# Expert weights loaded in fewer transfers with longer runs, in a fused attention and feed-forward kernel

## The chip, the cores and the metric

The kernel runs on one core of a Trainium2 chip. A core has five engines with instruction streams of their own: TensorE (PE, with weight loads shown apart as PEld), VectorE (DVE), ScalarE (ACT), GpSimd (POOL) and SyncE (SP). They meet through semaphores. Data comes from the chip's memory by DMA: here POOL issues all loads that turn float32 into float16 on the way, and SP issues the rest (stores, transposes, copies within the on-chip memory). The metric is the device time of one execution in microseconds; lower is better.

## What is computed

Attention over 8 batches with 8 heads of size 64: 512 local rows see 32 global columns and a band of 32 to each side; 32 global rows see everything. Its output, 4352 rows of 512 numbers, goes through a feed-forward layer whose activation is `h * clip(h + 3, 0, 6) / 6`.

```python
s_g = scale * q_g @ concat(k_g, k_l).T;  out_g = softmax(s_g) @ concat(v_g, v_l)
s_ll = where(abs(i - j) <= 32, scale * q_l @ k_l.T, -1e9)
out_l = softmax(concat(scale * q_l @ k_g.T, s_ll)) @ concat(v_g, v_l)
x = concat(out_g, out_l) as 4352 x 512
h = x @ w_in                       # w_in  512 x 2048
g = h * clip(h + 3, 0, 6) / 6
out = g @ w_out                    # w_out 2048 x 512
```

The inputs are float32; the kernel works in float16 with float32 sums.

## The kernel before

**A planner writes the order.** The kernel describes its work as operations with an engine (or a choice of engines), a cost, dependencies and a rank. `Plan.run` plays these through an event model and so fixes the order in which every engine gets its instructions; the code is then emitted in that order by hand (`tc.manual_schedule`). Each engine runs its own list strictly in order. So any change of a cost or a rank moves instructions on all engines, far from the edit. The semaphore waits are not the planner's: they are added when the program is built, from the regions of the tiles that instructions write and read.

**Loads.** `load` (L343) is a DMA issued by POOL, with a price from `dma(rows, run)` (L331): so many rows, each a run of so many bytes of float32. POOL's loads go through one queue, first in, first out, and at most eight are under way: a ninth waits for the first to land. The order of the first loads is the list `ORDER` (L379), read by `nth`: `k0 q0 v0 v1` are batch 0's, `K Q V G` batch 1's, `w0` to `w3` the quarters of w_in, `o0` to `o7` the eighths of w_out, `id` and `bd` the identity and the mask band.

**Weights.** `weights_in` (L637) loads w_in by quarters of its columns: 512 columns for each of the 512 rows, which are folded into 4 x 128 partitions, so 512 runs of 2 KB. `weights_out` (L643) loads w_out by 256 rows at a time, 256 runs of 2 KB.

**The feed-forward layer.** The 2048 hidden columns are cut into 16 groups of 128. `first` (L946) computes one group for up to 512 rows of x: four matmuls (L953) whose stationary side is a 128 x 128 piece of w_in, then a ReLU on ScalarE (L959) and a gate on VectorE (L963) that writes `g`. `second` (L970) multiplies all 16 groups with w_out (L979), four at a time. `ffn_local` (L1003) runs `first` for the 16 groups of a batch, for batch 0 in two halves of 256 rows; a group of w_in's quarter c depends on that quarter through `wi[c // (NDFF // 4)]` (L1012). `ffn_global` (L1028) does the 256 global rows at the end.

**Around the start.** Until the first x is ready, PE runs filler matmuls on the identity (L1094, `warm`), so that its clock stays up. Batch 0's attention uses scores (L769), maxima with the mask (L781), exponentials (L785), transposes of the probabilities (L798), products with v (L812), normalization (L824, L826) and a transpose of x (L833) that is copied to `xt`. Copies of v into strips (L630 on ScalarE, L632 on VectorE and POOL) may go to any of three engines in batches 0 and 1: the planner takes the one that is free.

## Time and profile before

| | |
|---|---|
| median of 3 runs | 334.06 us (333.06 to 334.21) |
| profiled execution, its time | 335.02 us |
| profiled execution, its span | 333.2 us |
| first w_in matmul starts (L953) | 29.66 us |
| first w_out matmul starts (L979) | 58.51 us |
| expert matmuls on 512 columns (L953, L979), mean of one as recorded | 357 and 372 ns |
| w_in, 4 loads: issue on POOL, median to landing | 0.76 us, 10.1 us |
| w_out, 8 loads: issue on POOL, median to landing | 0.72 us, 11.0 us |
| bytes moved, mean rate over the span | 42.10 MB, 126 GB/s |

The time is that of the whole execution; the span runs from the first to the last instruction, 1.8 us less. Matmuls are pipelined: a matmul of 512 columns is recorded with some 370 ns, but four of them follow each other in 0.86 us, so about 216 ns is what one takes from PE. A PE that is busy all the time on the page may therefore still have small gaps. The DMA view counts bytes as they are written, so a load that turns float32 into float16 shows half of what it reads.

### The profile page before, as it was taken

What the parts mean: (1) busy time and instruction counts of PE and PEld (TensorE: products, weight loads), DVE (VectorE), ACT (ScalarE), POOL (GpSimd) and SP (SyncE); (2) the same over time, 40 slices, a digit from 0 to 9 for tenths busy, and PEclk for the clock granted to TensorE, in tenths of its full rate; (3) what the DMA queues carried; (4) which work ended last, traced back from release to release, by engine and by line L of the source; (5) the groups of instructions that cost most, each with busy time, mean ns of one, the idle gap of its engine ahead of it and who ended that gap; (6) DMA issues with size and microseconds to landing.
All of it is one profiled execution on the core that took longest, in us unless ns stands there. A gap on an engine that the chain in (4) does not pass through costs nothing.

```text
span 333.2 us, 12723 instructions
## 1 busy us (share of the span) xinstructions
PE 319.2 (96%) x5101; PEld 165.7 (50%) x5101; DVE 247.2 (74%) x1003; ACT 232.1 (70%) x556; POOL 190.2 (57%) x299
## 2 busy tenths in 40 slices
PE   8998879899999999989999999999999999999996
PEld 3445656455455554545445444443444444446644
DVE  4799998798998689978977886779777873444400
ACT  4799998788988598889869658836278632535502
POOL 8687899997059989959999799794000000000000
PEclk9999997999999999999999999999999999999999
DMA  8999999891669999699944996799557671100013
GB/s 132 223 205 199 221 209 132 172 197 52 99 70 160 189 89 164 82 132 170 167 109 86 128 164 109 123 151 195 100 125 140 97 103 41 63 31 33 31 49 110
DMA packets 106059, 42.10 MB, mean 126 GB/s; under 512 B 84112, under 2 KB 101776, under 8 KB 106000
## 3 DMA queue, kind: packets, MB, share of 16 engines
q0 software_dynamic: 53136, 17.47, 52.8%
q1 hardware_dynamic: 52864, 23.82, 38.3%
q8 instruction: 40, 0.66, 0.8%
q14 instruction: 19, 0.16, 0.2%
HBM read 35.13 MB, written 8.91 MB: 132 GB/s over the span
## 4 chain that ended last, share of the span: by engine, by line
PE 76%; DVE 15%; DMA 4%; issue 2%; ACT 2%; ACTq 0%; DVEq 0%
PE m L979 26%; PE m L953 23%; PE t L979 7%; PE t L953 5%; DMA xt<-x 4%; DVE gl L963 4%; DVE vs L632 4%; PE m L1094 3%; PE s L769 3%; PE a L812 3%; DVE sm L781 2%; PE t L798 2%; DVE x L826 1%; DVE gm L882 1%; PE s L687 1%
## 5 line engine op out<-in xcount | busy, mean ns | idle before, releaser
L632 POOL COPY vs<-vn 32x528 f16<-32x528 f16 (+1 forms) x186 | 116.3, 625 | 12.2 <-ACT vn L372 1.0
L953 PE MATMUL m<-xt,win 128*128 128x512 f16 (+1 forms) x504 | 111.3, 357 | 3.5 <-DMA xt<-x 1.0
L979 PE MATMUL m<-wout,gl 128*128 128x512 f16 (+1 forms) x448 | 107.1, 372 | 0.1
L963 DVE SCALAR_TENSOR_TENSOR gl<-t,m 128x512 f16<-128x512 f32 (+1 forms) x139 | 81.2, 597 | 35.1 <-ACT t L959 34.1
L959 ACT ACTIVATE t<-m 128x512 f32<-128x512 f32 (+1 forms) x139 | 72.3, 531 | 44.6 <-PE m L953 40.2
L785 ACT ACTIVATE ex<-sm,mx 128x128 f16<-128x128 f32 x256 | 83.2, 396 | 9.6 <-DVE mx L781 8.9
L953 PEld LDWEIGHTS <-win 128*128 128x128 f16 x640 | 60.4, 99 | 57.1 <-issue 4.7
L979 PEld LDWEIGHTS <-gl 128*128 128x128 f16 x560 | 52.2, 98 | 54.6
L781 DVE CUSTOM_DVE_ANT_0 sm<-s,mask 128x128 f32<-128x128 f32 x256 | 58.9, 285 | 8.3 <-PE s L769 8.2
L979 PE MATMUL t<-wout,gl 128*128 128x512 f16 x112 | 28.8, 379 | 0.0
L826 DVE TENSOR_TENSOR x<-a,rec 128x256 f16<-128x256 f32 x64 | 24.1, 418 | 0.0
L344 POOL DMA_DIRECT2D vn<-in_v_l_dram x24 | 21.1, 898 | 0.5 <-issue 0.5
L781 DVE DVE_READ_ACCUMULATOR2_ANT mx<- 128x1 f32 x256 | 21.2, 83 | 0.0
L990 ACT COPY ot<-m 128x512 f32<-128x512 f32 (+1 forms) x21 | 11.9, 565 | 13.3 <-PE m L979 13.3
L959 ACT ACTIVATE t<-t 128x512 f32<-128x512 f32 (+1 forms) x21 | 11.9, 568 | 11.2 <-PE t L953 9.5
L963 DVE SCALAR_TENSOR_TENSOR gl<-t,t 128x512 f16<-128x512 f32 (+1 forms) x21 | 13.6, 647 | 8.1 <-ACT t L959 8.0
L953 PE MATMUL t<-xt,win 128*128 128x512 f16 x72 | 18.5, 379 | 0.4 <-DVE gl L963 0.4
L769 PE MATMUL s<-kT,qT 64*32 64x128 f16 x1024 | 14.4, 219 | 3.6 <-issue 3.0
L372 ACT COPY et<-t 128x1024 f16<-128x1024 f16 x16 | 16.2, 1012 | 0.9 <-PE t L798 0.9
L632 DVE COPY vs<-vn 64x528 f16<-64x528 f16 (+1 forms) x37 | 16.0, 431 | 1.0
L344 POOL DMA_DIRECT2D vn<-in_v_g_dram x7 | 4.1, 585 | 20.8 <-PE a L915 20.8
L769 PEld LDWEIGHTS <-qT 64*32 64x32 f16 x1024 | 8.2, 91 | 15.1 <-issue 14.5
(103 smaller groups left out, 309.7 us busy)
## 6 DMA issues: line engine op xcount, KB each, us to landing
out_dram<-ot SPq DMA_DIRECT2D x31, 256.0 KB, 2.7
vs<-vn SPq DMA_DIRECT2D x14, 264.0 KB, 7.2
kn<-in_k_l_dram POOLq DMA_DIRECT2D x14, 256.0 KB, 8.9
qn<-in_q_l_dram POOLq DMA_DIRECT2D x14, 256.0 KB, 6.6
vn<-in_v_l_dram POOLq DMA_DIRECT2D x24, 128.0 KB, 6.0
win<-in_moe_w_in_dram POOLq DMA_DIRECT2D x4, 512.0 KB, 10.1
wout<-in_moe_w_out_dram POOLq DMA_DIRECT2D x8, 256.0 KB, 11.0
gl<-in_v_l_dram POOLq DMA_DIRECT2D x8, 128.0 KB, 8.2
```

What stands on the lines that cost most here:

```text
L344: op = add("POOL", dma(rows, run), lambda: nc.gpsimd.dma_start(out=dst, in_=src), deps, rank, LOAD_LAT, what=what)
L372: nc.scalar.copy(out=dst(), in_=src())
L632: (nc.vector if o.on == "DVE" else nc.gpsimd).tensor_copy(out=dst, in_=src)
L769: nc.tensor.matmul(out=pss[e][u * Sg:(u + 1) * Sg, p * P:(p + 1) * P], lhsT=qT[r][rows, j, p, u * Sg:(u + 1) * Sg], rhs=kT[r][rows, p, k0: ...
L781: nc.vector.tensor_tensor_reduce(out=sm[i3][h], in0=pss[e][:, p * P:(p + 1) * P], in1=m, scale=-scale, scalar=3.0e38, op0=ALU.add, op1=ALU ...
L785: nc.scalar.activation(out=ex[ie][:, h, :], in_=sm[i3][h], func=EXP, scale=-1.0, bias=mx[i3][h])
L826: nc.vector.tensor_tensor(out=xs[ix][:, 4 * c * D:4 * (c + 1) * D].rearrange("q (h d) -> q h d", d=D), in0=acc[c][:, :, 0:D], in1=rr[c].to ...
L953: nc.tensor.matmul(out=ps[:, 0:n], lhsT=w_in[:, m, c * P:(c + 1) * P], rhs=x(m), start=(m == 0), stop=(m == NP - 1))
L959: nc.scalar.activation(out=t1[st["t"]][:, 0:n], in_=pm[st["m"]][:, 0:n], func=RELU, bias=0.5, scale=1.0 / 6.0)
L963: nc.vector.scalar_tensor_tensor(out=g, in0=t1[st["t"]][:, 0:n], scalar=1.0, in1=pm[st["m"]][:, 0:n], op0=ALU.min, op1=ALU.mult)
L979: nc.tensor.matmul(out=pm[st["m"]][:, 0:n], lhsT=g[c][:, t0:t0 + P], rhs=w_out[:, c, cols], start=(c == 0), stop=(c == NDFF - 1))
L990: nc.scalar.copy(out=ot[st["o"]][:, 0:n], in_=pm[st["m"]][:, 0:n])
```

## The change

```diff
-    ORDER = "k0 q0 v0 id v1 w3 K o5 o2 w2 V w0 o4 G bd w1 Q o0 o3 o7 o1 o6".split()
+    WI, RO = 2, 4
+    ORDER = "k0 q0 v0 id v1 w1 K o2 o1 V w0 G bd Q o0 o3".split()
...
+    w_in_c = w_in.rearrange("p m (g q i) -> p m g i q", q=P, i=RO)
+
     def weights_in():
-        part = dff // 4
+        part = dff // WI
         return [[load(w_in[:, :, c * part:(c + 1) * part],
                       moe_w_in[:, c * part:(c + 1) * part].rearrange("(m p) f -> p m f", p=P),
-                      NP * P, part * 4, [], nth(f"w{c}"), "win")] for c in range(4)]
+                      NP * P, part * 4, [], nth(f"w{c}"), "win")] for c in range(WI)]
 
     def weights_out():
         ops = []
-        for c in range(0, NDFF, 2):
-            ops += 2 * [load(w_out[:, c:c + 2, :], moe_w_out[c * P:(c + 2) * P, :].rearrange("(c p) f -> p c f", p=P),
-                             2 * P, dm * 4, [], nth(f"o{c // 2}"), "wout")]
+        for g in range(NDFF // RO):
+            ops += RO * [load(w_out[:, g * RO:(g + 1) * RO, :].rearrange("p i f -> p (i f)"),
+                              moe_w_out[g * RO * P:(g + 1) * RO * P, :].rearrange("(p i) f -> p (i f)", i=RO),
+                              P, RO * dm * 4, [], nth(f"o{g}"), "wout")]
         return ops
...
-                nc.tensor.matmul(out=ps[:, 0:n], lhsT=w_in[:, m, c * P:(c + 1) * P], rhs=x(m),
+                nc.tensor.matmul(out=ps[:, 0:n], lhsT=w_in_c[:, m, c // RO, c % RO], rhs=x(m),
                                  start=(m == 0), stop=(m == NP - 1))
...
-                deps = x_op[b][j0:j1] + wi[c // (NDFF // 4)]
+                deps = x_op[b][j0:j1] + wi[c * WI // NDFF]
```

w_in comes in two loads of half its columns, 512 runs of 4 KB each. w_out comes in four loads of 512 rows; four rows that follow each other in memory go to one partition, so a load is 128 runs of 8 KB. With that, partition p of w_out's group 4g + i holds hidden row 512g + 4p + i. So that `first` writes its hidden columns in the same numbering, the stationary side of its matmul takes every fourth column of w_in: 128 columns with a step of 4, from 512g + i. The list of the first loads names two halves `w0 w1` and four quarters `o0` to `o3`, in a new order. The planner gets new prices for the loads and so writes a new order for all engines. What is multiplied and added is the same.

## The prediction

> **What bounds the kernel now.** I read the page's busy shares first, then busy time by stretch, then the order of instructions around the first w_in matmul, then the landing of each weight transfer.

> ```profile
> PE 319.2 (96%) x5101; PEld 165.7 (50%) x5101; DVE 247.2 (74%) x1003; ACT 232.1 (70%) x556; POOL 190.2 (57%) x299
> ```

> The average says TensorE. By stretch it is two kernels (columns: PE, PEld, DVE, ACT, POOL busy, clock, DMA share, GB/s):

> ```profile
> 20.00:30.00 10.00, 8.50 (x176) 4.69 (x175) 9.79 (x51) 9.41 (x25) 9.42 (x16) 1.00 1.30 203
> 30.00:40.00 10.00, 8.83 (x211) 6.84 (x209) 9.76 (x28) 9.04 (x22) 7.31 (x11) 1.00 1.30 208
> 40.00:50.00 10.00, 7.27 (x168) 5.35 (x168) 9.48 (x30) 9.77 (x24) 9.58 (x18) 1.00 1.24 216
> ...
> 80.00:100.00 20.00, 20.00 (x422) 10.31 (x421) 18.71 (x69) 17.91 (x42) 6.24 (x10) 1.00 0.59 74
> ...
> 160.00:200.00 40.00, 40.00 (x662) 19.25 (x660) 33.08 (x133) 28.75 (x69) 35.44 (x55) 1.00 1.28 124
> ```

> To about 58 us VectorE and ScalarE are full (9.5 to 9.8 and 9.0 to 9.8 of 10) and the DMA queues too; after that PE never rests. So a microsecond lost by all three engines before 58 us is found again at the end: nothing later is idle enough to win it back. Useful PE work begins with the first expert matmul; before it PE runs filler (L1094):

> ```profile
> 28.71 0.10 PEld L953 LDWEIGHTS <-win 128*128 128x128 f16 x1
> 29.66 0.60 PE L953 MATMUL m<-xt,win 128*128 128x256 f16 x4 [0.88 <-DVE xt L374]
> ```

> The reader is to see that the weights were in at 28.7 us and that the matmul waited for x (the copy to xt), not for a DMA.

> **When weights land.** Issue time from the order of POOL's instructions, time to landing from the DMA view of that issue alone. The quarters of w_in are issued in the order w3, w2, w0, w1; the three below are w3, w0, w1:

> ```profile
> 6.86 0.79 POOL L344 DMA_DIRECT2D win<-in_moe_w_in_dram  x1
> 21.37 0.76 POOL L344 DMA_DIRECT2D win<-in_moe_w_in_dram  x1
> 27.78 0.77 POOL L344 DMA_DIRECT2D win<-in_moe_w_in_dram  x1
> ```

> ```profile
> win<-in_moe_w_in_dram POOLq DMA_DIRECT2D x1, 512.0 KB, 10.9
> win<-in_moe_w_in_dram POOLq DMA_DIRECT2D x1, 512.0 KB, 9.3
> win<-in_moe_w_in_dram POOLq DMA_DIRECT2D x1, 512.0 KB, 7.5
> ```

> So w3 lands at 17.8, w0 at 30.7, w1 at 35.3 us. POOL's queue is first in, first out and never empty here. Counted in the float32 bytes read (512 KB in SBUF is 1 MB read), w3 ends the 4th MB, the second K load the 5th (8.54 issued, 11.7 to land: 20.2), w0 the 9th, w1 MB 10.7. From 5 to 9 MB is 10.5 us: 2.6 us per MB; from 9 to 10.7 it is 2.7.

> **The change, part by part.**

> *A new wait, the main term.* In the built program before, the first matmul group of w_in (columns 8, w2's first) waits for w2 alone, and the groups of w3, w0 and w1 for theirs. In the changed program the first w_in weight load waits for two DMA counts: that of half w1 (columns 8 to 15) and, though it reads none of it, that of half w0, which is issued nine loads later. Its read now has a step of 4, and both halves lie in every row of the tile; presumably the tracking of the tile takes them to overlap. No later group waits for w_in. So the expert stage starts when w0 has landed. Ahead of it in the queue stand, in MB: k0 q0 v0 v1 3, w1 2, K 1, o2 o1 2, V 1; w0 makes 11. K then ends MB 6 at 20.2 + 2.6 = 22.8, and w0 comes 5 x 2.6 = 13 later: 35.8 us. POOL can issue w0 when K's first load has landed (about 21.5), well before its turn, so the queue doesn't run dry. The start moves from 29.66 to 35.8: **+6.1 us**. Bounds: longer runs are nowhere in the trace. Fastest: the GB/s row peaks at 250 against 205, 20% faster for the 6 MB of weights, -2.6 us. Slowest: the last five w_out loads take 9 us for 2.5 MB, 3.6 us per MB; at that pace w0's 2 MB cost 2 us more. So +3.5 to +8.1. I take 6.1, since the intervals of 1 MB and 0.5 MB loads show one pace.

> What is queued behind it: all of PE (the score matmuls of the global rows, the fourth transpose of probabilities, the third attention product, V of batch 1), ScalarE from its first gate (with four exponentials of batch 0's last block behind it), and VectorE from its first gate. VectorE reaches that gate at about 29.5: before it was 32.0, and three strip copies (0.31 each by their pitch), a normalization (0.95) and a copy of et (0.6) no longer stand ahead. So it idles some 7 us; POOL and DMA go on, but nothing there was what limited.

> *The clock.* PE will be idle for some 7 us. What that does:

> ```profile
> 49.50:51.00 1.50, 0.35 (x19) 0.25 (x19) 0.60 (x3) 1.46 (x3) 1.50 (x3) 1.00 1.65 163
> 51.00:52.50 1.50, 1.50 (x11) 1.17 (x12) 1.46 (x12) 1.12 (x4) 1.30 (x2) 0.71 1.69 114
> 52.50:54.00 1.50, 1.50 (x9) 1.03 (x7) 0.96 (x6) 1.08 (x5) 1.50 (x3) 0.50 1.76 109
> 54.00:55.50 1.50, 1.50 (x28) 0.97 (x34) 1.44 (x8) 1.35 (x6) 1.50 (x4) 0.66 2.02 140
> ```

> After a hole of 1.8 us the clock fell to a half; 16 expert matmuls took 3.35 us (52.08 to 55.43), against 16 x 0.109 = 1.75 at the pace of 8 in 0.87 later. Such a stretch after 35.8 costs +1.6. But the hole at 48.9 (1.77 us for which the trace shows no releaser, taken to be the supply of instructions) with its own 1.6 may go, since supply catches up during the wait: 0 to -3.4. I take half, -1.7: together **0**, from -1.8 to +1.6.

> *POOL.* Twelve weight issues (4 x 0.77 + 8 x 0.72 = 8.8 us) become six; a half has as many rows as a quarter, a w_out load half as many, so at most 6 x 0.79 = 4.7: 4 us of POOL time free before 36 us. In the new order POOL takes three more strip copies of batch 0, VectorE two and ScalarE one fewer; for batch 1 POOL takes five fewer and VectorE five more. VectorE: 3 x 0.31 = +0.9, in the stretch where it is the bound. Against that stand transposes of batch 2 that the new order puts ahead of the first w_out matmul (two q copies on VectorE, 1.3), and the start of the experts that x would have allowed earlier, which the wait swallows. Sum **0**, from -1.5 to +2. If POOL's time were not covered, its saving would still only bring loads nearer that wait behind the same queue.

> *Weight loads with a step of 4.* 640 loads read every fourth column. The trace has such reads once, the permutation (L455, step 4, 32 columns):

> ```profile
> 6.75 0.35 PEld L455 LDWEIGHTS <-ident 128*32 128x32 f16 x16
> ```

> Sixteen in 0.35 us, less the 0.13 of the last: 14 ns per 32 columns, 58 ns per 128. It must fit under a matmul of 512 columns (216 ns) or 256 (108): **0**, the cover being the matmul. Upper end: four times the 63 ns pitch of contiguous loads (eight of L798 in 0.54 us) is 252: 36 ns beyond 216 for 512 matmuls (18 us) and 144 beyond 108 for the 64 of the global rows (9 us). Lower end 0: loads are already hidden.

> *w_out* in fewer, longer pieces: its first use is at 58.5 us, its last part lands now at 45.9, in the new queue about MB 14: 35.8 + 3 x 2.7 = 44. Even 6 us later nobody waits: 0. PE's work is the same apart from three fillers.

> **Sum.** 6.1 + 0 + 0 + 0. The profiled execution has a span of 333.2 and a time of 335.02: it would be 339.3 and 341.1. The median of the three runs is 334.06, 0.96 below; so **340.2 us**.

> **Rivals.** *Swallowed in part (0.12).* VectorE, ScalarE and PE regain some, because the hole at 48.9 and its slow stretch go wholly (-3.4) and the copies come out at -1.5: 334.06 + 6.1 - 4.9 = 335.3. For it: PE has 7.3 of 10 at 40 to 50. Against: VectorE and ScalarE have 9.5 and 9.8 there.

> *The halves are early (0.06), the other side.* If each load carried an overhead that fewer loads save, w0 could be in before 29.7, and then the wait is free. Needed: 8 MB after v1's 3 MB (about 15.2) in 14.5 us, 1.8 us per MB. Then the experts start when x allows; x's copy has three strip copies and four maxima (0.21 each) fewer before it, 1.8 us: 334.06 - 1.8 = 332.3. It decides at a landing of 29.7. Against: K's and w_out's 0.5 MB loads land 1.0 to 1.3 us apart, the pace of 1 MB loads, so overheads overlap already. [...]

> *Stepped weight loads show (0.06).* Halfway to the upper end on the global rows alone, 64 x 0.07 = 4.5, with the wait: 344.7; the full 27 gives 367. Against: the 14 ns.

> **How the numbers follow.** The forecast has 0.76; its own range, the bounds of the wait, the clock and the order added as squares (3.5 below, 3.3 above), is 336.7 to 343.5. Down to the swallowed case the range is 335.2 to 343.5; left out are the other two rivals and the tails, some 2 in 10. What a measurement here can tell from no change is about 0.5%, 1.7 us: slower begins at 335.7, faster below 332.4. Slower: 0.76 + 0.06 and a third of the swallowed case, 0.86; same: the rest of it and a third of the early case, which lies at the edge, 0.10; faster 0.04.

> **What would show it.** First w_in matmul at 35 to 36.5, PEld or PE idle before it some 7 us, released by the w_in DMA; VectorE and ScalarE idle at 30 to 36; clock near 0.5 just after; PE without holes from about 65 us. Wrong if that matmul starts by 30, if its wait is there and the end isn't later, or if loads of w_in exceed 108 ns apart on the global rows.

## The result, and the profile after

The changed kernel takes 350.19 us (median of 4 runs, 348.77 to 350.31), against 334.13 (333.06 to 337.96, 4 runs) for the kernel before in the same session: a ratio of 1.0426, 95% interval 1.0366 to 1.0486. Medians here are of all runs; ratios leave out the few runs recorded as slow. It is slower by some 16 us; 6.1 were forecast, and the time lies above the range. The profiled execution took 350.31 us, its span is 348.3, 15.1 more than before.

From the page of the changed kernel:

```profile
PE 322.6 (93%) x5098; PEld 174.5 (50%) x5098; DVE 245.2 (70%) x1002; ACT 232.8 (67%) x559; POOL 183.8 (53%) x291
```

No engine has more work that matters. So the 15 us are idle time, and the list of waits of PE in the changed kernel (us in total, times, longest) has two that were not there before:

```profile
PE m L958 <- DMA win<-in_moe_w_in_dram: 8.5, 1, 8.5
PE a L692 <- issue: 4.5, 2, 3.5
```

L958 is the w_in matmul (L953 before), L692 the transposes of q and k (L687 before). "Issue" means that no semaphore is seen to release the engine. The kernel before has waits of that kind as well, but in its scores, 1.77 us at 48.9 us and 1.20 us at 64.1 us:

```profile
PE s L769 <- issue: 3.0, 2, 1.8
```

The timeline of PE in the changed kernel shows both waits in their places (start, length, what, and in brackets the idle time ahead):

```profile
35.30 2.72 PE L958 MATMUL m<-xt,win 128*128 128x256 f16 x12 [8.48 <-DMA win<-in_moe_w_in_dram]
...
66.07 0.35 PE L692 MATMUL a<-ident,kn 64*64 64x64 f16 x20
69.90 0.80 PE L692 MATMUL a<-ident,kn 64*64 64x64 f16 x44 [3.48 <-issue]
70.63 2.53 PE L958 MATMUL m<-xt,win 128*128 128x256 f16 x12
```

The first w_in matmul starts at 35.30 and was released by the load of w_in, as forecast. The second stop was not forecast: 20 of 64 transposes of k of batch 2 run, PE stands for 3.5 us, the other 44 run, and then 12 matmuls take 2.53 us that take 1.50 five microseconds earlier in the same timeline. The same by stretch (columns: PE, PEld, DVE, ACT, POOL busy, clock, DMA share, GB/s), changed kernel:

```profile
20.00:30.00 10.00, 6.49 (x136) 3.54 (x134) 8.39 (x50) 7.52 (x20) 8.80 (x15) 1.00 1.20 207
30.00:33.00 3.00, 0.00 (x0) 0.00 (x0) 0.00 (x0) 0.00 (x0) 0.94 (x2) 0.81 1.14 215
33.00:36.00 3.00, 0.70 (x4) 0.55 (x5) 0.00 (x0) 0.00 (x0) 0.30 (x1) 0.50 1.43 189
36.00:39.00 3.00, 3.00 (x54) 2.01 (x53) 1.67 (x5) 2.00 (x7) 2.78 (x5) 0.56 1.17 219
...
66.00:70.00 4.00, 0.53 (x30) 0.34 (x32) 1.91 (x13) 1.82 (x7) 3.66 (x6) 0.92 1.25 198
70.00:74.00 4.00, 4.00 (x93) 2.99 (x94) 1.91 (x5) 1.76 (x6) 3.88 (x8) 0.65 0.45 46
80.00:100.00 20.00, 20.00 (x448) 11.43 (x436) 17.71 (x90) 18.05 (x46) 6.54 (x11) 1.00 0.21 61
```

From 30 to 35 us all three engines that bounded this stretch before stand still, with 189 to 215 GB/s of DMA beside them; the clock falls to a half, stays there after the start (0.56), and falls again behind the second stop (0.65). From 80 to 100 us PE is full, as before: there is no room to win anything back. The loads themselves, from the view of the tile w_in and from the list of DMA issues of the changed kernel:

```profile
L958 PEld LDWEIGHTS <-win x640: 110/113/152, 35.3 to 330.7; 128*128 128x128 f16 x160
L344 POOL DMA_DIRECT2D win<-in_moe_w_in_dram x2: 747/764/782, 6.8 to 21.9; - x2
```

```profile
win<-in_moe_w_in_dram POOLq DMA_DIRECT2D x2, 1024.0 KB, 13.4
wout<-in_moe_w_out_dram POOLq DMA_DIRECT2D x4, 512.0 KB, 14.2
```

The halves are issued at 6.8 and 21.9 us and take 13.5 and 13.2 to land: 20.3 and 35.2. So the half w1, the one that the first w_in matmul reads, was there 15 us before the matmul was let go by the other half.

### The profile page after: what moved, and what is told of

The parts are those of the page before. It is cut to its first block, busy times and chain, and to the rows that moved or that the text cites. A ratio compares the mean times of both kernels' runs of the same rounds, so it can differ in the third digit from the quotient of the medians.

```text
span 348.3 us, 12696 instructions
## 1 busy us (share of the span) xinstructions
PE 322.6 (93%) x5098; PEld 174.5 (50%) x5098; DVE 245.2 (70%) x1002; ACT 232.8 (67%) x559; POOL 183.8 (53%) x291
## 4 chain that ended last, share of the span: by engine, by line
PE 79%; DVE 6%; DMA 5%; ACT 4%; issue 3%; POOL 2%; ACTq 0%; POOLq 0%
PE m L984 29%; PE m L958 26%; PE t L958 5%; PE t L984 5%; DMA win<-in_moe_w_in_dram 4%; PE s L774 3%; PE a L817 3%; PE t L803 2%; DVE gl L968 2%; DMA kn<-in_k_l_dram 1%; POOL vs L633 1%; ACT t L964 1%; PE a L692 1%; PE m L1099 1%; DVE vs L633 1%
## 5 line engine op out<-in xcount | busy, mean ns | idle before, releaser
L633 POOL COPY vs<-vn 64x528 f16<-64x528 f16 (+1 forms) x184 | 114.6, 623 | 20.2 <-ACT vn L372 9.3
L958 PE MATMUL m<-xt,win 128*128 128x512 f16 (+1 forms) x492 | 111.2, 360 | 11.5 <-DMA win<-in_moe_w_in_dram 8.5
L984 PE MATMUL m<-wout,gl 128*128 128x512 f16 (+1 forms) x480 | 118.2, 376 | 0.0
L964 ACT ACTIVATE t<-m 128x512 f32<-128x512 f32 (+1 forms) x134 | 70.5, 532 | 58.5 <-PE m L958 57.9
L958 PEld LDWEIGHTS <-win 128*128 128x128 f16 x640 | 69.7, 115 | 59.9 <-issue 14.4
L790 ACT ACTIVATE ex<-sm,mx 128x128 f16<-128x128 f32 x256 | 83.9, 395 | 10.1 <-DVE mx L786 9.9
L964 ACT ACTIVATE t<-t 128x512 f32<-128x512 f32 (+1 forms) x26 | 14.5, 557 | 14.0 <-PE t L958 13.8
L968 DVE SCALAR_TENSOR_TENSOR gl<-t,t 128x512 f16<-128x512 f32 (+1 forms) x26 | 16.5, 633 | 8.4 <-ACT t L964 8.3
L958 PE MATMUL t<-xt,win 128*128 128x512 f16 x84 | 21.6, 380 | 0.0
L344 POOL DMA_DIRECT2D vn<-in_v_l_dram x24 | 21.1, 896 | 0.1
L344 POOL DMA_DIRECT2D vn<-in_v_g_dram x7 | 4.1, 586 | 28.5 <-DVE rec L932 20.5
L984 PE MATMUL t<-wout,gl 128*128 128x512 f16 (+1 forms) x80 | 18.7, 358 | 0.0
L372 ACT COPY et<-t 128x1024 f16<-128x1024 f16 (+1 forms) x16 | 15.8, 985 | 2.2 <-PE t L803 1.6
L817 PE MATMUL a<-vs,et 128*32 128x65 f16 x1024 | 14.7, 195 | 2.5 <-DVE x L831 1.3
L817 PEld LDWEIGHTS <-et 128*32 128x32 f16 x1024 | 10.5, 96 | 11.8 <-issue 7.7
## 6 DMA issues: line engine op xcount, KB each, us to landing
win<-in_moe_w_in_dram POOLq DMA_DIRECT2D x2, 1024.0 KB, 13.4
wout<-in_moe_w_out_dram POOLq DMA_DIRECT2D x4, 512.0 KB, 14.2
```

The source lines that it names most:

```text
L344: op = add("POOL", dma(rows, run), lambda: nc.gpsimd.dma_start(out=dst, in_=src), deps, rank, LOAD_LAT, what=what)
L372: nc.scalar.copy(out=dst(), in_=src())
L633: (nc.vector if o.on == "DVE" else nc.gpsimd).tensor_copy(out=dst, in_=src)
L790: nc.scalar.activation(out=ex[ie][:, h, :], in_=sm[i3][h], func=EXP, scale=-1.0, bias=mx[i3][h])
L817: nc.tensor.matmul(out=psa[h // 4][q, c0:c0 + D + 1], lhsT=et[k][:, h * P + u * Sg:h * P + (u + 1) * Sg], rhs=vs[r][:, j * UJ + u, h, 0:D ...
L958: nc.tensor.matmul(out=ps[:, 0:n], lhsT=w_in_c[:, m, c // RO, c % RO], rhs=x(m), start=(m == 0), stop=(m == NP - 1))
```

## The experiments

Line numbers of the versions made from the changed kernel are its own up to L958; each diff is against the kernel named. Where a version is compared with another, the ratios are each to the kernel before in the same session.

### Two tiles for w_in

Against the changed kernel. Each half has a tile of its own; loads, order of the loads, steps of 4 and, instruction for instruction, the order on every engine are those of the changed kernel. Only the waits differ.

```diff
-    w_in = sb("win", [P, NP, dff])
+    w_in = [sb(f"win_{c}", [P, NP, dff // 2]) for c in range(2)]
...
-                nc.tensor.matmul(out=ps[:, 0:n], lhsT=w_in_c[:, m, c // RO, c % RO], rhs=x(m),
+                nc.tensor.matmul(out=ps[:, 0:n], lhsT=w_in_c[c // RO // PW][:, m, c // RO % PW, c % RO], rhs=x(m),
```

> The changed kernel with w_in in two tiles, one per half; every load, every read with a step of 4 and the order on every engine stay, but the first w_in matmul waits for half w1 alone. Theory A, the wait for the wrong half is the whole loss: the first w_in matmul starts at 27.5 to 28.5 us, the first w_out matmul at 56 to 60, 332 to 336 us in all. Theory B, the wait is worth only its 5.6 us at the start (35.30 against 29.66) and the rest, some 10 us, comes from the new order: 342 to 345 us. Theory C, the stepped weight loads (113 ns for 98) cost by themselves: above 336 with the global rows' matmul groups further apart than 0.87 us per 8.

Measured: 336.34 us, ratio 1.0032 (0.9986 to 1.0077), span 333.2. PE's timeline of the version with two tiles:

```profile
26.75 1.47 PE L958 MATMUL m<-xt,win 128*128 128x256 f16 x12
...
43.91 0.49 PE L692 MATMUL s<-ident,qn 64*64 64x64 f16 x35 [1.11 <-issue]
```

The loss is gone, all of it. Halves, longer runs, stepped weight loads and the new order together cannot be told from no change; without the wait for a half that is not read, none of the loss is left. One number was not foreseen: without the wait the experts start at 26.75, 2.9 us before those of the kernel before (29.66), and yet nothing is gained. The first w_out matmul comes at 59.75 against 58.51: between the first w_in and the first w_out matmul the new order puts 635 matmuls where the old one has 483, among them 128 more transposes of q and k and 32 more products with v.

### The wait put back alone

Against the version with two tiles: one matmul of 1 column that reads half w0, ahead of the first w_in matmul.

```diff
+            if touch and touch.pop():
+                nc.tensor.matmul(out=ps[:, 0:1], lhsT=w_in[0][:, 0, 0:P], rhs=ident[:, 0:1])
             for m in range(NP):
```

> The version with w_in in two tiles (1.0032 of before, first w_in matmul at 26.7 us) with one more matmul of 1 column, put ahead of the first w_in matmul, which reads half w0; the output is unchanged, since the next matmul starts that bank afresh. Theory (the wait for w0 is the whole loss of the changed kernel): the start moves back to 35.3 us or close by, and the time to that of the changed kernel less nothing, 1.035 to 1.05 of before; if the 3.5 us hole in the k transposes at 66 us comes from the wait and not from that kernel's one tile, it is back too, and without it the ratio is some 1.028. Rival (the single tile costs something else too, such as waits later on): 1.01 to 1.025 with the same start.

Measured: 348.27 us, ratio 1.0378 (1.0309 to 1.0447), span 347.7. PE's timeline of this version (its L959 is the added matmul, L961 the w_in matmul):

```profile
36.44 0.19 PE L959 MATMUL m<-ident,win 128*128 128x1 f16 x1 [8.51 <-DMA win<-in_moe_w_in_dram]
36.48 1.87 PE L961 MATMUL m<-xt,win 128*128 128x256 f16 x8
...
67.18 0.35 PE L692 MATMUL a<-ident,kn 64*64 64x64 f16 x19
70.12 0.55 PE L692 MATMUL a<-ident,kn 64*64 64x64 f16 x45 [2.60 <-issue]
```

One wait, and the loss is back, with the second stop in the same transposes: after 19 of 64 instead of 20. The list of PE is one matmul longer here, and the stop came one matmul sooner. That became the clue to what the second stop is (below).

### Keeping w0 out of the way by order

Against the changed kernel: w0 right behind w1 among the loads.

```diff
-    ORDER = "k0 q0 v0 id v1 w1 K o2 o1 V w0 G bd Q o0 o3".split()
+    ORDER = "k0 q0 v0 id v1 w1 w0 K o2 o1 V G bd Q o0 o3".split()
```

> The changed kernel with half w0 loaded right behind half w1; one tile, so the wait for both stays, but w0 is then the 7th MB and lands at about 25.5 us, before x is ready. Theory A: no wait at the first w_in matmul, 333 to 338 us, with K and V 5 us later than in the changed kernel without harm. Theory B (the order costs): 340 or more. Theory C as for the two tiles.

Measured: 342.95 us, 1.0228 (1.0152 to 1.0304), span 341.3. The start moved to 27.6 us and w_out's first matmul to 46.2; about half of the loss is gone, the rest is lost elsewhere. The same holds for two further orders without that wait: quarters of w_in in four tiles with the quarters of w_out as in the changed kernel (start 29.1), and two tiles with V ahead of the w_out quarters, tried as a version that might beat both (start 27.1).

```diff
-    WI, RO = 2, 4
-    ORDER = "k0 q0 v0 id v1 w1 K o2 o1 V w0 G bd Q o0 o3".split()
+    WI, RO = 4, 4
+    ORDER = "k0 q0 v0 id v1 w3 K o2 w2 V w0 G bd w1 Q o1 o0 o3".split()
```

> w_out in four loads with runs of 8 KB, w_in read with a step of 4, but w_in still in four quarters with runs of 2 KB, each in a tile of its own, so that no matmul waits for a quarter that it doesn't read. Theory A, only the wait for the wrong part costs: 333 to 337 us. If runs of 8 KB or stepped reads cost: above 338.

```diff
-    ORDER = "k0 q0 v0 id v1 w1 K o2 o1 V w0 G bd Q o0 o3".split()
+    ORDER = "k0 q0 v0 id v1 w1 K V w0 o2 G bd Q o1 o0 o3".split()
```

> Two tiles for w_in, and V and w0 two loads earlier, the w_out quarters later: order k0 q0 v0 id v1 w1 K V w0 o2 G bd Q o1 o0 o3. A try at a version that is better than both. Theory: V late is what leaves PE a hole at 44 us in the version with two tiles; with V earlier the start stays near 26.7 and the time comes to 0.99 to 1.00 of before. Rival (every new order makes the planner place work anew, and stalls of instructions with half clock behind them come at other places, as in three of four orders tried): 1.01 to 1.035.

Measured: 344.89 us, 1.0242 (1.0190 to 1.0295), and 344.90 us, 1.0268 (1.0168 to 1.0368). The busy time from 120 to 130 us, first the quarters, then w0 second, then V early, and last the version with two tiles, where nothing is lost:

```profile
120.00:130.00 10.00, 5.91 (x248) 4.27 (x249) 7.01 (x35) 8.60 (x19) 8.03 (x12) 0.82 1.30 169
```

```profile
120.00:130.00 10.00, 7.09 (x132) 3.92 (x136) 7.87 (x55) 7.00 (x20) 9.80 (x15) 0.66 1.95 182
```

```profile
120.00:130.00 10.00, 5.48 (x151) 3.09 (x150) 6.06 (x47) 7.05 (x20) 9.55 (x14) 0.76 1.48 187
```

```profile
120.00:130.00 10.00, 10.00 (x187) 5.58 (x164) 9.50 (x37) 7.51 (x16) 9.17 (x15) 1.00 1.10 149
```

Three of these four orders without the wait lose 3 to 4.5 us of PE there, with a lowered clock beside it; the kernel before and the version with two tiles lose none. A start that is 2 us earlier is worth less than what a planned order happens to do a hundred microseconds later. The timelines show there waits for maxima on VectorE (up to 1.3 us), for ScalarE (1.5, quarters), for a transfer of xt (1.9, with V early) and, with w0 second, a stop of the kind that is explained below (1.8, and another one at 141 us); why these orders meet them and the others don't was not followed further.

### Halves without the step

Against the kernel before: w_in by halves with contiguous reads (so that the waits are exact with one tile), w_out in eight loads as before.

```diff
-    ORDER = "k0 q0 v0 id v1 w3 K o5 o2 w2 V w0 o4 G bd w1 Q o0 o3 o7 o1 o6".split()
+    ORDER = "k0 q0 v0 id v1 w1 K o5 o4 o2 o3 V w0 G bd Q o0 o1 o6 o7".split()
...
-        part = dff // 4
+        part = dff // 2
```

> w_in in two halves with runs of 4 KB, read without a step in one tile, w_out in eight loads as before: the built program waits for each half by itself. Theory A: 333 to 338 us, first w_in matmul at 26 to 29 us. If halves as such cost, because K, V and the second half land later: above 339.

Measured: 349.26 us, 1.0368 (1.0316 to 1.0419), span 347.9, start 26.7. The waits of PE in this version:

```profile
PE m L953 <- DVE gl L963: 8.3, 10, 2.2
PE m L979 <- issue: 2.8, 1, 2.8
PE m L953 <- issue: 1.9, 1, 1.9
```

As slow as the changed kernel, for reasons of its own: waits for the gate, 8.3 us, and two stops without a releaser, at 113 and 191 us. As a test of halves it is a miss: the order that it needed changed too much to tell the halves from the order. One thing it does show: with halves in one tile but without the step, the first w_in matmul starts at 26.7 us and doesn't wait for w0. So it takes the step and the common tile together to make the wait.

### What the late start costs by itself

Two pairs put fillers ahead of the first w_in matmul, large ones that hold PE and keep its clock, and small ones (1 column) that add only the instructions. In the changed kernel 36, in the kernel before 26:

```diff
+            for _ in range(fill.pop() if fill else 0):
+                nc.tensor.matmul(out=ps, lhsT=ident, rhs=ident[:, 0:1].to_broadcast([P, 512]))
             for m in range(NP):
```

> The changed kernel with 36 filler matmuls (7.8 us) in front of its first w_in matmul, which fill the time that it waits anyway (26.8 to 35.3 us): the wait stays, the clock doesn't fall in it. If the half clock after the hole is part of the loss (clock 0.50 to 0.56 from 33 to 39 us and 0.58 again at 45 to 48), 2 to 5 us come back: 345 to 348. If it is not, 350.

> The changed kernel with 36 filler matmuls of one column in front of its first w_in matmul: as many instructions as with 36 fillers of 512 columns, hardly any work, so PE's instruction list is shifted alike but the clock falls in the wait. Theory, the clock made the 6 us of that run: about 350 us as the changed kernel, clock near 0.5 from 33 us. Rival, the shift of the instruction list made them (it moved the 3.5 us hole without a releaser at 66 us): 344 to 346.

> The kernel before with 26 filler matmuls of 512 columns (5.6 us) in front of its first w_in matmul: a pure delay of the size of the start's shift, with the clock kept up; loads unchanged. The prediction's arithmetic, delay passes one to one: 339.7 us. Rival, a hole at this place grows by itself (waits of the following stage line up badly): 344 or more. Second rival, part is won back: under 338.

> The kernel before with 26 filler matmuls of one column in front of its first w_in matmul: the instruction list is shifted as with 26 fillers of 512 columns, the start is 0.7 us later at most. If the delay made that run's 8 to 9 us: 335 us. If the shifted list did (its 3.9 us hole without a releaser at 64.6 us and the slow clock behind it): 338 to 342, with that hole present.

| version | median | ratio | first w_in, w_out matmul |
|---|---|---|---|
| changed, 36 large | 344.18 us | 1.0270 (1.0196 to 1.0344) | 35.9, 70.0 us |
| changed, 36 small | 346.42 us | 1.0281 (1.0229 to 1.0333) | 35.5, 71.0 us |
| before, 26 large | 343.80 us | 1.0267 (1.0194 to 1.0340) | 34.5, 62.4 us |
| before, 26 small | 338.82 us | 1.0056 (1.0012 to 1.0100) | 29.6, 58.3 us |

By stretch, changed kernel with large fillers, then with small ones:

```profile
33.00:36.00 3.00, 2.30 (x13) 0.93 (x11) 0.00 (x0) 0.00 (x0) 0.00 (x0) 1.00 1.42 189
36.00:39.00 3.00, 3.00 (x63) 2.63 (x62) 1.99 (x6) 2.40 (x8) 2.71 (x5) 1.00 1.19 219
```

```profile
33.00:36.00 3.00, 0.50 (x3) 0.41 (x4) 0.00 (x0) 0.00 (x0) 0.09 (x1) 0.50 1.43 190
36.00:39.00 3.00, 3.00 (x53) 1.90 (x52) 1.46 (x4) 1.79 (x6) 2.98 (x5) 0.50 1.16 215
```

A clock of 1.00 instead of 0.50 brings the first w_out matmul 1.0 us forward (70.0 against 71.0), although the w_in matmuls begin 0.4 us later; the ratios can't tell the two apart. So the slow clock in the wait is worth about 1 us. What both share, 72 more instructions on PE, is worth more: the 3.5 us stop is gone, idle times of 1.6 (large) and 1.1 us (small) ahead of the first w_out matmul stand in its place, and the ratio of the changed kernel falls from 1.0426 to 1.0270 and 1.0281. In the kernel before, the same kind of edit does the opposite: its stop of 1.77 us goes, and that of 1.20 grows to 3.5. Its timelines, with small and with large fillers:

```profile
59.76 0.72 PE L687 MATMUL a<-ident,kn 64*64 64x64 f16 x59
63.97 0.23 PE L687 MATMUL a<-ident,kn 64*64 64x64 f16 x5 [3.49 <-issue]
```

```profile
63.87 0.72 PE L687 MATMUL a<-ident,kn 64*64 64x64 f16 x59
68.47 0.23 PE L687 MATMUL a<-ident,kn 64*64 64x64 f16 x5 [3.87 <-issue]
```

Four microseconds apart in time, both stop after the same 59 of 64 transposes. So the place of a stop is a place in the list, not a moment. As for the delay itself: between small and large fillers the kernel before starts its w_in matmuls 4.9 us later and its ratio rises by 2.1%, some 7 us. The intervals leave about 3 us either way, so this pair can't decide whether a plain delay costs more than itself.

### What the stop is

PE's list is numbered as built, weight loads included (the matmul that is the k-th of the trace, counted from 0, has number 2k + 2). The first matmul after the longest stop without a releaser has the number 1726 in the kernel before (in the scores at 48.9 us), 1982 in the changed kernel, 1982 with the wait put back, 2238 in the kernel before with 26 fillers of either kind, 1470 in the version with two tiles. These differ by 256 or a multiple of it. (The two stops of the halves without the step stand one and four matmuls ahead of 4286 and 7102, which belong to the same series; by then the trace shows 4 and 11 semaphore instructions between PE's matmuls that the count leaves out.) The queues of the page hold the other half:

```profile
q8 instruction: 40, 0.66, 0.9%
```

The planner of both kernels reckons with such blocks. `Plan.fetch` (L58) counts PE's instructions by 256; in its model a block comes a fixed time after PE nears the end of the block ahead of it, longer when loads are under way. These times are constants of the code, which no run here measures. `pick` (L1122, L1127 in the changed kernel) puts an expert matmul in place of small ones that would stop for more than 0.1 us in this model. So PE's order is laid out around these stops, for the times of the plan. In the plan of the changed kernel the first w_in matmul depends on half w1 alone (L1017); the 8.5 us that it really waits are not in it. That the stop of 3.5 us comes of this difference is likely, but no run tests it.

To test the blocks, the version with two tiles got more instructions for the same work: some of the 58 fillers ahead of the first w_in matmul were cut in two, 30 of them in one version and 48 in the other.

```diff
+    split = [[slice(0, 512)]] * 40 + [[slice(0, 256), slice(256, 512)]] * 30
...
-            nc.tensor.matmul(out=pm[slots["m"][0]], lhsT=w, rhs=x)
+            for h in split.pop():
+                nc.tensor.matmul(out=pm[slots["m"][0]][:, h], lhsT=w, rhs=x[:, h])
```

> The version with w_in in two tiles, with 30 of the 58 fillers ahead of the first w_in matmul cut in two (2 x 256 columns for 512): the same work, 60 more instructions on PE. What the traces so far show: every hole of over a microsecond for which no releaser is shown stands at the same place of PE's instruction list, counted by 256 instructions (1726 before, 1982 in the changed kernel and in the one with the read of w0, 2238 in before with 26 small fillers, 1470 in the two tiles), and ends 1.2 to 1.6 us after a 16 KB transfer of the instruction queue. Theory (the list comes in blocks of 256, the next block asked for when PE enters the one before, and usable some 5.8 us after that): with 60 more, the borders stand at other work, which takes 5.5 to 9.4 us for each block in the stretch of 25 to 70 us. The 1.3 us hole at 42.6 us and the lower clock behind it go, no hole over 0.6 us stands before 80 us, and the ratio is 0.988 to 1.000. Rival (the holes come from what the DMA queues do at that time, wherever PE is): a hole near 43 us again, 1.003 as before.

> The same with 48 fillers cut in two, 96 more instructions. Theory: the borders now stand where PE runs through a block of short matmuls in 3.4 to 4.1 us. Holes of 1.5 to 2.5 us are to be seen in the global rows' attention products (L920, after 38 of 40) at about 45 us and in the scores (L774, after 25 of 32) at about 58 us, with a lower clock behind them, and none at 42.6; the ratio is 1.003 to 1.02, and the time 1.5 to 6 us over that of the version with 30. Rival (place in the list doesn't matter): the two versions agree within 0.5%.

Measured: with 30, 338.27 us, 1.0078 (1.0043 to 1.0113); with 48, 344.85 us, 1.0284 (1.0236 to 1.0332). PE's timeline with 48:

```profile
42.56 0.32 PE L817 MATMUL a<-vs,et 128*32 128x65 f16 x17 [0.48 <-ACT kT L372]
43.92 0.31 PE L817 MATMUL a<-vs,et 128*32 128x65 f16 x15 [1.04 <-issue]
...
46.13 0.48 PE L920 MATMUL a<-vn,et 128*32 128x65 f16 x37
50.39 0.24 PE L920 MATMUL a<-vn,et 128*32 128x65 f16 x3 [3.79 <-issue]
...
62.94 0.36 PE L774 MATMUL s<-kT,qT 64*32 64x128 f16 x24
65.50 0.25 PE L774 MATMUL s<-kT,qT 64*32 64x128 f16 x8 [2.20 <-issue]
```

The places came out to within one matmul: after 37 of 40 (38 forecast) and after 24 of 32 (25 forecast); the trace shows two semaphore instructions ahead of them, which is one matmul with its load. The rival, that place doesn't matter, falls: the same work in the same order differs by 2% between 30 and 48 cuts. The sizes and the times did not come out: 3.8 us where 1.5 to 2.5 were forecast, a stop at 42.9 where none was, the second one some 5 us later in time, and +2.8% where +2% was the most. With 30 cuts the stop near 43 us is gone as forecast, but the forecast of no stop over 0.6 us before 80 us failed twice. A gap of 0.96 us stands at number 2238 (62 us; shown as a wait for ScalarE, yet its end is 1.4 us behind a transfer). And the cuts bring a border, number 448, into scores of batch 0:

```profile
12.52 0.30 PE L774 MATMUL s<-kT,qT 64*32 64x128 f16 x15
14.45 0.32 PE L774 MATMUL s<-kT,qT 64*32 64x128 f16 x17 [1.62 <-issue]
```

This stop ends 1.5 us behind a transfer too. In the version with two tiles these 32 scores start at 12.54 us and run through, and the filler behind them starts 1.8 us earlier than here. That is the whole of the late start with 30 cuts, 28.55 us for 26.75, and so nothing is won. (With 48 cuts the same place stops for 0.70 us.) These places show that the stops stand at such numbers, and the records that they end 1.2 to 1.6 us behind a transfer; that PE waits for the transfer is inferred from the two. When the next block is asked for, and what its transfer waits for, is not shown: ahead of the stops of the kernel before it started 2.9 and 3.3 us after PE entered the block before, ahead of those of the changed kernel 5.0 and 4.1, and the DMA shares don't explain which (1.3 us in the version with two tiles and 5.0 in the changed kernel for the same block, with the DMA engines about equally full: shares of 1.5 to 1.9 and 1.8 to 2.0).

## Why the prediction fell short

The changed kernel and the version with two tiles run the same list on PE, so that their delay can be read instruction by instruction from the records (number in PE's list, delay in us):

| at | delay | what was added |
|---|---|---|
| 896, first w_in matmul | 8.55 | the wait for w0 |
| 1214 | 10.27 | +1.7, half clock behind the wait: +1.4 to 38.7 us, -0.7, then +1.0 in a second stretch of it from 45.5 us |
| 1470 | 8.76 | -1.5, most of it a stop that only the two tiles have here |
| 1726 | 9.54 | +0.8 |
| 1982 | 13.27 | +3.7, the stop at the block's border |
| 2238 | 14.16 | +0.9, half clock behind it |
| end | 15.03 | +0.87: -0.55 by number 4000, +1.24 up to and with a stop at the border 4030 (118.8 us), +0.18 later |

Both the version with two tiles and the kernel before have a span of 333.2. So the 15.1 us against the kernel before are: the start, 35.30 for 29.66, +5.6; the head start of 26.75 that the new order had and lost, +2.9; and what the delay brought after the start, 15.03 - 8.55 = +6.5.

**The wait: right in mechanism and size.** Forecast: a new wait of the first w_in load for half w0, start at 35.8 us, +6.1, released by the w_in DMA, VectorE and ScalarE idle from 30 to 36. Found: 35.30, +5.6, and the idle engines. The landing of w1, the 5th MB, comes out at 20.2 by the prediction's count and was 20.3. That the step of 4 makes the read of one half wait for the other was presumed in the prediction; the two tiles (step, no wait) and the halves without the step (one tile, no wait) show it together.

**The order and POOL: the term that was mis-sized, 0 (-1.5 to +2), measured +2.9.** In the prediction's words, "the start of the experts that x would have allowed earlier, which the wait swallows" was counted as a gain not had, at nothing. But with that earlier start the new order only comes out even (1.0032): it has 152 more small matmuls between the first w_in and the first w_out matmul. Take the start away, and these are still there. That they are what eats the head start is argued, not shown. Here the head start that the wait swallowed was a loss against the old order, not a zero.

**The clock and the stop: the step that failed, 0 (-1.8 to +1.6), measured +6.5.** The slow clock after the wait was forecast at +1.6 and is +1.7 here (about 1 by the large fillers); that it fits is in part luck, since the figure holds two stretches of half clock and a regain of 0.7 between them. The stop of 1.77 us at 48.9, of which the prediction took half to go on the presumption that instructions catch up in the wait, did go: PE passes 1470 and 1726 without one. It was treated as a stop that is there or not; it stood at 1726, one of a series of numbers 256 apart. The next stop came at 1982 and was twice as long: PE ran through the block before it, transposes and scores of batch 2 among expert matmuls, in 4.2 us (62.1 to 66.2), and the transfer of the next one started only 5.0 us after PE had entered that block. The version with two tiles runs through the same block in 4.1 us without a stop, its transfer having started after 1.3; what held the other back stays open. The profile of the kernel before had shown a second such stop, 1.20 us at 64.1 us and 512 numbers behind the first; the prediction says of that stretch that PE "never rests", and didn't price it. "PE without holes from about 65 us" was wrong for the same reason. This also speaks against the rival that the delay is swallowed in part: on balance nothing was regained, and the price was more than the shift of the start, 15 us for 5.6.

**Weight loads with a step of 4: right that they cost nothing, with the cover named.** One took 113 ns for 98 before, but they lie beside matmuls (108 and 216 ns each) that PE does meanwhile: the 64 matmuls of 256 columns on the global rows follow each other, within a group of w_in, every 109 ns in the kernel before, the changed kernel and the version with two tiles alike, and the last of these has the time of before. **Halves early: wrong, as forecast.** A half took 13.4 us to land where a quarter took 10.1 (median), and all bytes together come at the same rate (207 to 208 GB/s against 203 to 208 between 20 and 40 us). Up to its end there are four loads fewer than the same bytes would make in quarters and eighths, and w0 came only 0.6 us sooner than forecast from the pace of the kernel before (35.2 for 35.8). **w_out: nothing, as forecast.**

## What to carry to other kernels

Read a stationary tile with a step where its parts, loaded one by one, lie in every row, and what is read may be taken to touch every part: look at which landing the first reader waits for, and give each part a tile of its own; here the one tile cost a wait of 8.5 us. When a wait is added, price it against the start that the new order would have had, not against the old kernel's. And where PE runs many small matmuls, a stop with no releaser is worth locating in the instruction list: if it sits at a fixed number and not at a fixed time, a delay or a few instructions more ahead of it can change it. In the changed kernel the stop of 1.77 us was gone and one of 3.48 stood 256 numbers later, and 26 tiny matmuls made 3.49 us of one of 1.20.

## What the runs showed of the hardware

- The stops of PE without a releaser that are numbered above stood at places of its list that lie 256 numbers, or a multiple of it, apart: 1726 and 2238 in the kernel before (1.77 and 1.20 us), 1982 and one matmul ahead of 4030 in the changed kernel (3.48 and 1.06), 1982 with the wait put back (2.60), 2238 in the kernel before with 26 fillers (3.49 and 3.87), 1470 in the version with two tiles (1.11). In the kernel before and the changed kernel these four ended 1.4 to 1.5 us behind a 16 KB transfer of the queue that the page calls instruction. Adding 26 tiny matmuls, with no other change, cost the kernel before 0.56% (0.12 to 1.00).
- The granted clock fell behind some short stops: to 0.65 from 70 to 74 us behind one of 3.48 us in the changed kernel, to 0.50 from 52.5 to 54 us behind one of 1.77 us in the kernel before, in a stretch of transposes and scores, and to 0.57 from 44 to 48 us behind one of 1.11 us in the version with two tiles. Behind the one of 1.20 us in the kernel before it stayed at 1.00 (64 to 72 us).
- Runs of 4 and 8 KB in place of 2 KB moved these loads no faster: 207 to 208 GB/s between 20 and 40 us, against 203 to 208 in the kernel before.
